# One run of full-array and one run of half-array matmuls in each mLSTM step

## The chip, the cores and the metric

The kernel runs on one core of a Trainium2 chip. The number that counts is the device time of one execution in microseconds. The engines are TensorE (PE in the rows, its weight loads PEld), VectorE (DVE), ScalarE (ACT), GpSimd (POOL) and SyncE (SP), which issues most of the transfers.

## What is computed

Three layers follow each other; only the first is touched by the change.

```python
# mLSTM: 4 batches x 8 heads, 768 time steps, head size 40
for t in range(S):
    m_new = np.maximum(f_gate[:, :, t] + m, i_gate[:, :, t])
    f_stab, i_stab = np.exp(f_gate[:, :, t] + m - m_new), np.exp(i_gate[:, :, t] - m_new)
    C = f_stab * C + i_stab * einsum('bhd,bhe->bhde', vt, kt)
    n = f_stab * n + i_stab * kt
    y[:, :, t] = sigmoid(o_gate) * (C @ qt) / max(|n . qt|, 1)
# routed layer on y as 3072 tokens of 320: 8 experts, one for each token
logits = x @ w_gate + modality_bias[modality_id]
e_idx = argmax(logits);  gate_w = softmax(logits)[e_idx]
out[mask_e] = gate_w * (relu(x[mask_e] @ w1[e]) @ w2[e])
# last layer: h = x @ w_in;  out = (h * cos(h)) @ w_out
```

## The kernel before

The recurrence is computed in chunks of 128 time steps: 6 chunks for each of 4 batches give 24 tiles of 128 tokens, and the main loop (`for i in range(NT)`, line 1070) runs over them, chunk by chunk and batch by batch. A tile holds all 8 heads in 4 pairs. The order of instructions on every engine is the order of the Python text (`manual_schedule`); the framework adds the waits. A step `i` of the loop is a software pipeline over several tiles. On TensorE it issues, in this order:

- `scores(i)`, line 459: products of queries and keys, in two groups of two head pairs. For each group two full-array matmuls (128 columns of weights, line 466) and four half-array ones (64 columns, line 472), into bank 0 for the first group and bank 1 for the second. A VectorE multiply (line 478) reads the bank of a group and follows it.
- in steps 8, 12 and 16 the count matmuls of `rank_mm` (line 656), full-array, into bank 7;
- `values(i - 1)`, line 482: the state update into bank 6 (line 491, half-array; VectorE adds it to the state in line 515), the values into bank 4 (line 498), the state's part into bank 5 (line 506; VectorE reads it in line 520). All of them are half-array;
- `spread_later(i + 2)`, line 250: the gates of a later tile, half-array, into bank 3, for ScalarE's exponentials (line 427);
- `xpose(i - 2)`, line 551: three full-array transposes of the finished tile, line 555, into bank 2;
- `logits(i - 3)`, line 560: six half-array matmuls, line 565, into columns 256 on of bank 6, read by VectorE in line 566.

A matmul of float32 leaves two records in the trace. The ranks are the tokens' places within their experts: after the tokens of a round (4 tiles, one chunk) are routed, `rank_mm(c)` counts on TensorE, and the generator `rank(c)` reads the counts on VectorE (line 677 first). Its further instructions are a background list, from which `fill()` takes one at a time at places in `scores` and `values`. Rounds 0 to 2 are ranked in steps 8, 12 and 16, round 3 through `weigh_later` in step 19, round 4 behind the loop in `first_slot`. After rounds 3 and 4 the count of each expert is left in columns 128 to 135 of the same bank, where `pick_first` and `pick_second` read it (lines 715 and 725): the two experts with the most tokens get their weights first. In steps 4, 5, 8, 9, 12 and 13 VectorE also unpacks pieces of the last layer's weights (`_decode`). SyncE loads the inputs of tile `i + 3` in step `i`; a buffer comes free when VectorE and TensorE have read it.

Of the kernel before, what the change touches and what calls it, by code (L numbers as in the profile page):

```python
# [8 lines left out]
F32 = mybir.dt.float32  # L9
# [5 lines left out]
ALU = mybir.AluOpType  # L15
# [4 lines left out]
B, H, S, D = 4, 8, 768, 40  # L20
L = 128
NC = S // L
# [3 lines left out]
NT = NTOK // 128  # L26
E = 8
# [68 lines left out]
def kernel(  # L96
# [362 lines left out]
    def scores(i):  # L459
        t = qk_t[i % NQ]  # L460
        P = st[i]
        for g in range(2):
            pairs = slice(2 * g, 2 * g + 2)
            sp = bk[g][:, 0:6 * HL].rearrange("p (n k t) -> p n k t", n=2, k=3)
            for m in range(2):
                T_.matmul(
                    out=sp[:, m, 0:2].rearrange("p k t -> p (k t)"), lhsT=t[:, 2 * g + m, HL:3 * HL],
                    rhs=t[:, 2 * g + m, QO:QO + L], start=True, stop=True,
                )
            for m in range(2):  # L470
                for a, z in enumerate(Z):
                    T_.matmul(
                        out=sp[z, m, 2], lhsT=t[:, 2 * g + m, 5 * a * HL:(5 * a + 1) * HL],
                        rhs=t[:, 2 * g + m, QO + HL:QO + L],
                        start=True, stop=True,
                    )
            pg = P[:, pairs, 0:3]
            V.tensor_tensor(out=pg, in0=sp, in1=pg, op=ALU.mult)
            if i > 1:
                fill(2)  # L480
# [78 lines left out]

    def logits(i):  # L560
        xT = xTt.pop(i)
        pl = bk[6][:, 256:256 + E] if i < NT - 2 else bk[3 if i < NT - 1 else 2][:, 0:E]
        for k in range(3):
            for z in (slice(0, 64), slice(64, 128)):
                T_.matmul(out=pl[z], lhsT=xT[:, k, z], rhs=wg[:, k, :], start=(k == 0), stop=(k == 2))
        V.tensor_tensor(out=lg[:, i, :], in0=pl, in1=bias[:, i, :], op=ALU.add)
        fill()
# [88 lines left out]
    def rank_mm(c):  # L656
        j0, n = c * B, B
        r = slice(j0, j0 + n)
        b_ = bk[7 if c < NC - 1 else 4]
        pk = b_[:, 64:64 + n * E]  # L660
        T_.matmul(out=pk, lhsT=trib[:, 0, :], rhs=oh[:, r].rearrange("p j e -> p (j e)"), start=True, stop=False)
        pk3 = pk.rearrange("p (j e) -> p j e", j=n)
        for j in range(n - 1):
            T_.matmul(
                out=pk3[:, j + 1:], lhsT=trib[:, 1, :],
                rhs=oh[:, j0 + j].unsqueeze(1).to_broadcast([128, n - 1 - j, E]), start=False, stop=False,
            )
        T_.matmul(
            out=pk3, lhsT=trib[:, 1, :], rhs=cum[:, c].unsqueeze(1).to_broadcast([128, n, E]), start=False, stop=True
        )  # L670
        if j0 + n in EARLY:
            T_.matmul(out=b_[:, 128:128 + E], lhsT=trib[:, 1, :], rhs=cum[:, c + 1], start=True, stop=True)
        return pk3

    def rank(c, pk3):
        r = slice(c * B, (c + 1) * B)
# [37 lines left out]

    def pick_first():
        r = m8[:, 1:2]
        yield from best(bk[7][:, 128:128 + E], m8[:, 0:1], r)
        V.tensor_scalar(out=tab0[:, 0:1], in0=r[0:1], scalar1=-1.0, scalar2=float(E), op0=ALU.mult, op1=ALU.add)
        yield
        V.tensor_scalar(out=star, in0=e8, scalar1=r, scalar2=None, op0=ALU.not_equal)  # L720
        yield
        V.tensor_scalar(out=s1, in0=e8, scalar1=r, scalar2=None, op0=ALU.is_equal)
        yield

    def pick_second():

        r = m8[:, 3:4]
        V.scalar_tensor_tensor(
            out=sc, in0=star, scalar=float(SLOT), in1=bk[7][:, 128:128 + E], op0=ALU.mult, op1=ALU.add
        )  # L730
        yield
        V.scalar_tensor_tensor(out=e8, in0=sc, scalar=2.0 * SLOT, in1=s1, op0=ALU.is_ge, op1=ALU.mult)
# [310 lines left out]
    def in_turn(*gs):  # L1043
        for g in gs:
            yield from g

    def weigh_later(c):
        if c < SLOW:
            wt[c] = weights(c)
            bg.append(wt[c])  # L1050
            return
        run(weights(c))
        wq.append(weigh(c))
        wt[c] = in_turn(rank(c, rank_mm(c)), rows_of(c))
        bg.append(wt[c])

    dec_ops = _decode(nc, (raw_t, dtu_t), w_in, w_out, w_ir, None, PIECES[:DA])
# [12 lines left out]
    for i in range(NT):  # L1070
# [8 lines left out]
        else:  # L1079
# [1 line left out]
            if i >= 4 and i < NT - 1 and (i - 4) % B == B - 1 and (i - 4) // B >= SLOW:  # L1081
                ex_exp((i - 4) // B)
            scores(i)
        if i >= 8 and i % B == 0 and i // B - 2 < SLOW:
            c = i // B - 2
            bg.append(in_turn(rank(c, rank_mm(c)), rows_of(c)))
        if i == NT - 2:
            run(e0)
            early_rows(0)
# [27 lines left out]
            next(gp)  # L1117
        if B <= i + 2 < NT:
            spread_later(i + 2)
        if i >= 2:  # L1120
            xpose(i - 2)
        if i >= 3:
            logits(i - 3)
        if i >= 3 and (i - 3) % B == B - 1:
            rt = route((i - 3) // B)
            bg.append(rt)
# [45 lines left out]
    twice(0)  # L1172

    def first_slot():
        rk_ = rank(NC - 2, rank_mm(NC - 2))
        bg.extend([in_turn(pick_second(), early_slot(1, sc)), in_turn(rk_, rows_of(NC - 2))])
        fill(14)
        for f in (1, 2):
            split_in(w1r, f, f, V, V, (1,))
        for _ in xpose_b(0, (4, 1, 0)):  # L1180
            fill(F0)
        for _ in range(2):
            next(we)
        split_out(w2r, 0, 0, V)
# [651 lines left out]
```

## Time and profile before

| | |
|---|---|
| median of 3 runs | 753.02 us (752.61 to 753.65) |
| the profiled execution | 751.96 us, span 750.2 us |
| TensorE busy | 719.6 us, 96% of the span |
| VectorE, ScalarE, GpSimd busy | 522.3, 387.1, 210.1 us |
| the 24 mLSTM steps | 7.75 to 151.75 us of the span |

The span runs from the first to the last instruction. In a timeline a row has its start, its duration, the engine, the line, operation and tiles, the shape of the weights (128\*128 is full-array, 128\*64 half-array) and the number of records merged; in brackets stands the idle time before it and what ended that. Spans of matmuls overlap, so their starts are to be compared, not their ends. A table by stretch has the length of a stretch, the busy time of each engine in it with the number of instructions, and the clock granted to TensorE as a share of 2.4 GHz. Steps are counted from 0; step 5 begins at 41.02 us and step 19 at 119.90.

### The profile page before, as it was taken

How to read it: one execution, taken by the hardware profiler on the slowest of the kernel's cores; microseconds unless marked ns; L12 is line 12 of the kernel's file. 1: busy time of each engine (PE TensorE's matmuls, PEld its weight loads, DVE VectorE, ACT ScalarE, POOL GpSimd, SP SyncE). 2: the span in 40 equal slices, each digit the busy share in tenths (PEclk: the TensorE clock that was granted, in tenths of full speed). 3: DMA queues.
4: the chain of work that ended last, by engine and by line, in shares of the span. 5: the costliest groups of instructions: out<-in, count | busy, mean ns of one | idle time of the engine just before them, and what ended most of it. 6: DMA issues, size and time to landing. Idle time of an engine off the chain costs nothing. (4 is left out here: it accounts for less than half of the span.)

```text
span 750.2 us, 16869 instructions
## 1 busy us (share of the span) xinstructions
PE 719.6 (96%) x6131; PEld 655.5 (87%) x6132; DVE 522.3 (70%) x1206; ACT 387.1 (52%) x910; POOL 210.1 (28%) x282
## 2 busy tenths in 40 slices
PE   8999999978999999999979999999999999999995
PEld 5888887868999999999868899998999999989994
DVE  7888888786456786773748867766767676667662
ACT  4666655463334555453736655555555555555551
POOL 7776674411344233421642002002002002001002
PEclk9999999999999999999989999999999999999998
DMA  7867877811345653423820011010010000000000
GB/s 188 220 192 206 216 211 209 249 66 54 110 125 151 206 172 98 117 71 114 267 74 1 1 35 36 1 36 36 0 36 36 1 1 36 0 1 19 18 1 35
DMA packets 45262, 68.42 MB, mean 91 GB/s; under 512 B 4846, under 2 KB 32944, under 8 KB 45168
## 3 DMA queue, kind: packets, MB, share of 16 engines
q1 hardware_dynamic: 37856, 45.16, 21.3%
q10 hardware_dynamic: 3664, 10.27, 4.7%
q0 software_dynamic: 3648, 11.82, 4.7%
q8 instruction: 49, 0.80, 0.5%
q14 instruction: 45, 0.37, 0.2%
HBM read 84.58 MB, written 12.14 MB: 129 GB/s over the span
## 5 line engine op out<-in xcount | busy, mean ns | idle before, releaser
L1648 ACT ACTIVATE w1r<-w1r 128x512 f32<-128x512 f32 x96 | 60.7, 632 | 104.3 <-DVE w1r L1643 104.3
L1650 DVE TENSOR_TENSOR w1r<-bk,w1r 128x512 f32<-128x512 f32 x96 | 66.3, 691 | 52.5 <-ACT w1r L1648 51.0
L1641 ACT ACTIVATE w1r<-bk,qtr 128x512 f32<-128x512 f32 x96 | 65.9, 687 | 57.9 <-PE bk L1636 57.8
L961 PE MATMUL bk<-XH,WIH 128*128 128x256 f32 x288 | 76.8, 296 | 1.9 <-DVEq L942 0.9
L1642 DVE TENSOR_SCALAR w1r<-w1r 128x512 f32<-128x512 f32 x96 | 41.1, 428 | 52.8 <-ACT w1r L1641 52.8
L967 ACT ACTIVATE hh<-bk 128x256 fp32r<-128x256 f32 x96 | 36.6, 381 | 77.2 <-PE bk L961 60.6
L1643 DVE TENSOR_TENSOR w1r<-w1r 128x512 f32<-128x512 f32 x96 | 68.7, 716 | 3.3
L1668 PE MATMUL bk<-WOH,gh 128*128 128x320 f32 x228 | 71.0, 311 | 0.0
L1668 PE MATMUL bk<-WOH,gl 128*128 128x320 f32 x228 | 70.5, 309 | 0.0
L1668 PE MATMUL bk<-WOL,gh 128*128 128x320 f32 x228 | 70.4, 309 | 0.0
L968 DVE SCALAR_TENSOR_TENSOR hl<-bk,hh 128x256 fp32r<-128x256 f32 x96 | 40.1, 418 | 40.9 <-ACT hh L967 29.7
L1636 PE MATMUL bk<-XH,WIH 128*128 128x512 f32 x144 | 58.3, 405 | 4.5 <-issue 3.8
L982 PE MATMUL bk<-WOH,hl 128*128 128x320 f32 x192 | 59.6, 311 | 0.9 <-DVE hl L968 0.9
L982 PE MATMUL bk<-WOH,hh 128*128 128x320 f32 x192 | 59.7, 311 | 0.0
L982 PE MATMUL bk<-WOL,hh 128*128 128x320 f32 x192 | 59.4, 309 | 0.0
L961 PEld LDWEIGHTS bk<-XH,WIH 128*128 128x128 f32 x288 | 54.8, 190 | 4.5 <-DVEq L942 3.4
L1636 PE MATMUL bk<-XL,WIH 128*128 128x512 f32 x144 | 57.8, 401 | 0.0
L988 POOL DMA_INDIRECT x_d<-ys,cinv x26 | 28.9, 1111 | 101.6 <-ACTq L942 72.5
L1636 PE MATMUL bk<-xh,WIH 128*128 128x512 f32 x144 | 56.5, 392 | 0.0
L1636 PE MATMUL bk<-xl,WIH 128*128 128x512 f32 x144 | 56.1, 389 | 0.0
L961 PE MATMUL bk<-XL,WIH 128*128 128x256 f32 x288 | 50.6, 284 | 2.7 <-DVE XL L867 2.7
L961 PE MATMUL bk<-XH,WIL 128*128 128x256 f32 x192 | 49.9, 282 | 0.0
(390 smaller groups left out, 1990.8 us busy)
## 6 DMA issues: line engine op xcount, KB each, us to landing
w2r<-in_w_dram SPq DMA_DIRECT2D x26, 640.0 KB
w1r<-in_w_dram SPq DMA_DIRECT2D x26, 512.0 KB
w1r<-in_w_dram SPq DMA_DIRECT2D x52, 128.0 KB
kvl<-in_kvn_dram SPq DMA_DIRECT2D x12, 484.0 KB
raw<-in_w_out_dram ACTq DMA_DIRECT2D x8, 640.0 KB
qkl<-in_qk_dram SPq DMA_DIRECT2D x24, 160.0 KB
x_d<-y SPq DMA_DIRECT2D x24, 160.0 KB
raw<-in_w_in_dram ACTq DMA_DIRECT2D x6, 512.0 KB
```

The source lines that it names most:

```text
L961: T_.matmul(out=ph, lhsT=a, rhs=x_, start=(n == 0), stop=(n == len(mms) - 1))
L967: A.activation(out=hh, in_=ph, func=AF.Relu)
L968: V.scalar_tensor_tensor(out=hl, in0=ph, scalar=0.0, in1=hh.bitcast(F32), op0=ALU.max, op1=ALU.subtract)
L982: T_.matmul(out=py(s, g), lhsT=a[:, gs], rhs=w_, start=(f == 0 and n == 0), stop=(f == NF - 1 and n == 2),)
L988: r = G_.indirect_dma_start(out=dst, out_offset=bass.IndirectOffsetOnAxis(ap=idx, axis=0), in_=src, in_offset=None, bounds_check=NTOK - 1, ...
L1636: T_.matmul(out=ph, lhsT=a, rhs=x_, start=(n == 0), stop=(n == len(mms) - 1))
L1641: A.activation(out=v, in_=gp[T, f], func=AF.Identity, bias=qtr, scale=1.0 / (2 * math.pi))
L1642: V.tensor_scalar(out=kk, in0=v, scalar1=MAGIC, scalar2=MAGIC, op0=ALU.add, op1=ALU.subtract)
L1643: V.tensor_tensor(out=v, in0=v, in1=kk, op=ALU.subtract)
L1648: A.activation(out=v, in_=v, func=AF.Sin, scale=6.283185)
L1650: V.tensor_tensor(out=g, in0=gp.pop((T, f)), in1=v, op=ALU.mult)
L1668: T_.matmul(out=po, lhsT=a[:, js], rhs=w_, start=(f == 0 and n == 0), stop=(f == NFC - 1 and n == 2),)
```

## The change

In `scores` the full-array matmuls of both groups go first, and then the half-array ones of both. `logits` goes ahead of `xpose`, and its output into bank 7 for tiles 2 to 20. The count matmuls of rounds 0 to 2 go behind `xpose`, and those of rounds 0 to 3 into bank 6. As bank 6 is also the state update's, the first VectorE instruction of `rank` follows the counts at once (`rank_first`), and the experts' counts are copied to a tile, `cnt`, which the picks read.

```diff
     def scores(i):
...
-        for g in range(2):
-            pairs = slice(2 * g, 2 * g + 2)
-            sp = bk[g][:, 0:6 * HL].rearrange("p (n k t) -> p n k t", n=2, k=3)
+        sps = [bk[g][:, 0:6 * HL].rearrange("p (n k t) -> p n k t", n=2, k=3) for g in range(2)]
+
+        for g, sp in enumerate(sps):
             for m in range(2):
                 T_.matmul(
                     out=sp[:, m, 0:2].rearrange("p k t -> p (k t)"), lhsT=t[:, 2 * g + m, HL:3 * HL],
                     rhs=t[:, 2 * g + m, QO:QO + L], start=True, stop=True,
                 )
+        for g, sp in enumerate(sps):
+            pairs = slice(2 * g, 2 * g + 2)
             for m in range(2):
                 for a, z in enumerate(Z):
...
     def logits(i):
         xT = xTt.pop(i)
-        pl = bk[6][:, 256:256 + E] if i < NT - 2 else bk[3 if i < NT - 1 else 2][:, 0:E]
+        if i < NT - 2:
+            pl = bk[7 if 1 < i < NT - 3 else 6][:, 256:256 + E]
+        else:
+            pl = bk[3 if i < NT - 1 else 2][:, 0:E]
...
     def rank_mm(c):
...
-        b_ = bk[7 if c < NC - 1 else 4]
+        b_ = bk[(6, 7, 4)[max(c - NC + 3, 0)]]
...
+    cnt = ra.tile([128, E], F32, name="cnt")
+
+    def rank_first(c, pk3):
+
+        g = rank(c, pk3)
+        next(g)
+        if (c + 1) * B in EARLY:
+            V.tensor_copy(out=cnt, in_=bk[6 if c < NC - 2 else 7][:, 128:128 + E])
+        return g
...
-        yield from best(bk[7][:, 128:128 + E], m8[:, 0:1], r)
+        yield from best(cnt, m8[:, 0:1], r)
...
-        wt[c] = in_turn(rank(c, rank_mm(c)), rows_of(c))
+        wt[c] = in_turn(rank_first(c, rank_mm(c)), rows_of(c))
...
             scores(i)
-        if i >= 8 and i % B == 0 and i // B - 2 < SLOW:
-            c = i // B - 2
-            bg.append(in_turn(rank(c, rank_mm(c)), rows_of(c)))
...
+        if i >= 3:
+            logits(i - 3)
         if i >= 2:
             xpose(i - 2)
-        if i >= 3:
-            logits(i - 3)
+        if i >= 8 and i % B == 0 and i // B - 2 < SLOW:
+            c = i // B - 2
+            bg.append(in_turn(rank_first(c, rank_mm(c)), rows_of(c)))
```

`pick_second` reads `cnt` in the same way, and `first_slot` calls `rank_first`. Line numbers behind `scores` grow by 2 to 15 with the change.

The order of the instructions is shown at three places, where `bk_77` and `bk_78` are banks 0 and 1, `bk_79` is bank 2, and `bk_83` and `bk_84` are banks 6 and 7. TensorE at the end of an ordinary step and the start of the next, before:

```order
L260 MATMUL bk_80<-g_108,pick 64x128
L555 MATMUL bk_79<-cst,y 128x128 x3
L565 MATMUL bk_83<-wg,xT_226 64x8 x6
L466 MATMUL bk_77<-qkl_123 128x128 x2
L472 MATMUL bk_77<-qkl_123 64x64 x4
L466 MATMUL bk_78<-qkl_123 128x128 x2
L472 MATMUL bk_78<-qkl_123 64x64 x4
L491 MATMUL bk_83<-kvl_124,kw_107 64x41 x8
```

and the same place after:

```order
L260 MATMUL bk_80<-g_108,pick 64x128
L570 MATMUL bk_84<-wg,xT_226 64x8 x6
L557 MATMUL bk_79<-cst,y 128x128 x3
L466 MATMUL bk_77<-qkl_123 128x128 x2
L466 MATMUL bk_78<-qkl_123 128x128 x2
L474 MATMUL bk_77<-qkl_123 64x64 x4
L474 MATMUL bk_78<-qkl_123 64x64 x4
L493 MATMUL bk_83<-kvl_124,kw_107 64x41 x8
```

The six matmuls of the logits moved past the transposes and into bank 7, and between the gates' last matmul and the state update there is now one run of each shape. TensorE in step 16, with the counts of round 2, before:

```order
L472 MATMUL bk_78<-qk_111 64x64 x4
L661 LDWEIGHTS trib
L661 MATMUL bk_84<-oh,trib 128x32
L664 LDWEIGHTS trib
L664 MATMUL bk_84<-oh,trib 128x24
L664 LDWEIGHTS trib
L664 MATMUL bk_84<-oh,trib 128x16
L664 LDWEIGHTS trib
L664 MATMUL bk_84<-oh,trib 128x8
L668 LDWEIGHTS trib
L668 MATMUL bk_84<-cum,trib 128x32
L491 MATMUL bk_83<-kvl_125,kw_105 64x41 x8
```

and after:

```order
L570 MATMUL bk_84<-wg,xT_226 64x8 x6
L557 MATMUL bk_79<-cst,y 128x128 x3
L666 LDWEIGHTS trib
L666 MATMUL bk_83<-oh,trib 128x32
L669 LDWEIGHTS trib
L669 MATMUL bk_83<-oh,trib 128x24
L669 LDWEIGHTS trib
L669 MATMUL bk_83<-oh,trib 128x16
L669 LDWEIGHTS trib
L669 MATMUL bk_83<-oh,trib 128x8
L673 LDWEIGHTS trib
L673 MATMUL bk_83<-cum,trib 128x32
```

The counts moved from behind the scores to the end of the step and from bank 7 to bank 6. VectorE between steps 19 and 20, from the last instruction of the round's weights to the state update, before:

```order
L613 RECIPROCAL gate<-gate 128x4
L478 TENSOR_TENSOR Pl_129<-bk_77,Pl_129 128x2x192
L677 TENSOR_TENSOR tot<-bk_84,oh 128x32
L706 TENSOR_REDUCE m_254<-bk_84 128x1
L478 TENSOR_TENSOR Pl_129<-bk_78,Pl_129 128x2x192
L679 TENSOR_REDUCE rk<-tot 128x4
L708 SCALAR_TENSOR_TENSOR e_255<-bk_84,m_254,cst 128x8
L515 TENSOR_TENSOR Ml_131<-Mc_215,bk_83 40x4x41 x2
```

and after:

```order
L618 RECIPROCAL gate<-gate 128x4
L692 TENSOR_TENSOR tot<-bk_83,oh 128x32
L687 COPY cnt<-bk_83 128x8
L480 TENSOR_TENSOR Pl_129<-bk_77,Pl_129 128x2x192
L694 TENSOR_REDUCE rk<-tot 128x4
L721 TENSOR_REDUCE m_255<-cnt 128x1
L480 TENSOR_TENSOR Pl_129<-bk_78,Pl_129 128x2x192
L696 TENSOR_SCALAR hF<-rk 128x4
L723 SCALAR_TENSOR_TENSOR e_256<-cnt,m_255,cst 128x8
L517 TENSOR_TENSOR Ml_131<-Mc_215,bk_83 40x4x41 x2
```

The read of the counts moved ahead of the scores' multiplies, and the copy to `cnt` stands behind it.

## Rows read from the trace of the kernel before

**Rows 1.** Busy time by stretch, steps 3 to 23; columns as described above.

```profile
28.30:41.02 12.72, 12.72 (x196) 10.89 (x195) 8.74 (x21) 8.74 (x28) 10.06 (x16) 0.89 0.70 198
41.02:63.36 22.34, 22.15 (x421) 19.41 (x418) 17.71 (x56) 12.70 (x48) 15.53 (x26) 1.00 0.71 202
63.36:86.00 22.64, 22.40 (x421) 19.53 (x417) 19.68 (x67) 13.91 (x50) 15.31 (x24) 1.00 0.80 222
86.00:108.66 22.66, 22.42 (x422) 19.54 (x418) 19.71 (x67) 13.39 (x48) 15.76 (x25) 1.00 0.77 207
108.66:119.90 11.24, 11.10 (x210) 9.64 (x206) 7.79 (x29) 6.74 (x25) 7.45 (x13) 1.00 0.75 202
119.90:133.16 13.26, 11.15 (x216) 9.73 (x212) 12.17 (x43) 6.96 (x25) 4.40 (x8) 1.00 0.80 222
133.16:151.75 18.59, 17.19 (x266) 15.00 (x262) 13.43 (x55) 8.12 (x28) 7.51 (x11) 0.91 0.88 252
```

**Rows 2.** Waits, 41.02 to 119.90: who for whom, total, times, longest (us).

```profile
DVE Ml L515 <- PE bk L506: 6.7, 6, 1.4
...
DVE M L515 <- PE bk L506: 4.6, 3, 1.6
...
PEld bk L491 <- DVE lg L566: 0.5, 3, 0.2
```

**Rows 3.** VectorE's waits, 63.36 to 86.00.

```profile
DVE Ml L515 <- PE bk L506: 2.2, 2, 1.4
```

**Rows 4.** Timeline of TensorE, step 18.

```profile
114.41 0.71 PE L466 MATMUL bk<-qkl 128*128 128x128 f32 x4
115.05 0.45 PE L472 MATMUL bk<-qkl 128*64 128x64 f32 x8
...
116.07 0.45 PE L472 MATMUL bk<-qkl 128*64 128x64 f32 x8
116.36 0.62 PE L491 MATMUL bk<-kvb,kw 128*64 128x41 f32 x16
...
118.85 0.55 PE L555 MATMUL bk<-cst,y 128*128 128x128 f32 x3
119.45 0.52 PE L565 MATMUL bk<-wg,xT 128*64 128x8 f32 x12
119.90 0.71 PE L466 MATMUL bk<-qkl 128*128 128x128 f32 x4
```

**Rows 5.** Timeline of TensorE, small windows: scores of step 17; the last gate matmul.

```profile
108.87 0.50 PE L466 MATMUL bk<-qkb 128*128 128x128 f32 x3
109.09 0.28 PE L466 MATMUL bk<-qkb 128*128 128x128 f32 x1
...
118.70 0.22 PE L260 MATMUL bk<-g,pick 96*64 96x128 bf16 x1
```

**Rows 6.** Line 466, 41 to 120: its weight loads, ns minimum/median/maximum.

```profile
L466 PEld LDWEIGHTS bk<-qkl x57: 186/189/192, 46.5 to 119.9; 128*128 128x128 f32 x57
```

**Rows 7.** Timeline of TensorE behind the loop: transposes, then a full-array matmul.

```profile
155.25 0.55 PE L555 MATMUL bk<-cst,y 128*128 128x128 f32 x3
155.55 0.37 PE L961 MATMUL bk<-XH,WIH 128*128 128x256 f32 x1
```

**Rows 8.** Timeline of VectorE between steps 19 and 20.

```profile
128.77 0.18 DVE L613 RECIPROCAL gate<-gate 128x4 f32<-128x4 f32 x1
...
130.72 0.66 DVE L515 TENSOR_TENSOR Ml<-Mc,bk 40x164 f32<-40x164 f32 x2 [0.45 <-PE bk L506]
```

**Rows 9.** Timeline of TensorE: step 20, scores of step 21, the last values.

```profile
128.34 0.62 PE L491 MATMUL bk<-kvl,kw 128*64 128x41 f32 x16
...
133.16 0.93 PE L466 MATMUL bk<-qkb 128*128 128x128 f32 x4
...
136.28 1.40 PE L498 MATMUL bk<-vb,Pl 128*64 128x82 f32 x21
...
151.75 1.14 PE L498 MATMUL bk<-vbl,Pl 128*64 128x82 f32 x21 [1.40 <-DVE lg L566]
```

More of the change, by code (lines that the diff above doesn't have):

```diff
@@ L728, in pick_second @@
         V.scalar_tensor_tensor(
-            out=sc, in0=star, scalar=float(SLOT), in1=bk[7][:, 128:128 + E], op0=ALU.mult, op1=ALU.add
+            out=sc, in0=star, scalar=float(SLOT), in1=cnt, op0=ALU.mult, op1=ALU.add
         )
@@ L1174, in first_slot @@
     def first_slot():
-        rk_ = rank(NC - 2, rank_mm(NC - 2))
+        rk_ = rank_first(NC - 2, rank_mm(NC - 2))
         bg.extend([in_turn(pick_second(), early_slot(1, sc)), in_turn(rk_, rows_of(NC - 2))])
```

## The prediction

> **What bounds the kernel now.** The change touches only the first fifth of the program, the 24 mLSTM steps, so I read the busy time by stretches first [rows 1]: in each stretch the reader is to set TensorE's busy time beside the length. From 41.02 to 119.90 us (steps 5 to 18) TensorE is busy for 22.15 of 22.34, 22.40 of 22.64, 22.42 of 22.66 and 11.10 of 11.24 us, at the full 2.4 GHz (granted clock 1.00). These steps are as long as TensorE's instructions are. VectorE is next: 17.71, 19.68, 19.71 and 7.79 us. The second and third stretch hold the steps in which VectorE also unpacks the late weights; there little is free on it. In 119.90 to 133.16 (steps 19 and 20) VectorE leads instead, 12.17 against 11.15 of 13.26.
>
> Second, the waits of VectorE, since they say how much of a TensorE gain it can follow. From 41.02 to 119.90 it waits for one thing, the matmuls of line 506, for 6.7 + 4.6 = 11.3 us [rows 2]; 2.2 us of that fall into 63.36 to 86.00 [rows 3], and the next stretch, 86.00 to 108.66, has the same busy time.
>
> Third, the timeline of TensorE in step 18, where nothing but the order of shapes costs time [rows 4]. The step lasts 119.90 - 114.41 = 5.49 us. Its scores take 116.36 - 114.41 = 1.95 us: a group of full-array matmuls 0.64 (115.05 - 114.41), a group of half-array ones, the same again, the last half-array group, which more half-array work follows, only 0.29. Inside a full-array group the pitch is small: its second record starts at 108.87 and its fourth at 109.09, so 0.11 us each [rows 5]. The rest of the 0.64 is paid on the way in and out of the group.
>
> **The change part by part.**
>
> *Scores.* The two full-array groups become one of eight records and the two half-array groups one of eight pairs. The first takes 0.64 + 4 x 0.11 = 1.08 us. The second takes 0.29 plus four more pairs at no more than 0.29 / 4 = 0.07; inside a run I take 0.06, so 0.24. Sum 1.61 against 1.95: 0.34 us less in each step, 0.29 at the least.
>
> A weight load of these matmuls takes 186 to 192 ns [rows 6], longer than the 0.11 us pitch, so it runs beside the matmul before it. The Trainium skill (TensorE: Matmul & The Clock Gate, Part 3, "The mechanism") says that a weight load overlaps running matmuls only where their row groups differ, which full-array ones never do. By that rule the four added records would cost 4 x 0.19 and the scores would gain 0.02 instead of 0.34; the pitch in the trace speaks against it, and I go by the pitch.
>
> *Logits ahead of the transposes.* Now: last gate-spreading matmul 118.70 [rows 5], transposes 118.85, logits 119.45, next scores 119.90 [rows 4]; 1.20 us. The logits start 0.60 after three transposes that elsewhere need 155.55 - 155.25 = 0.30 until a full-array matmul follows them [rows 7]. After the change: logits one half-array pitch behind the spreading (0.06), 0.45 from them to the transposes (what they take to the next full-array matmul now), 0.30 to the scores: 0.81. Saved 0.39. Part of it is a wait and not a switch: the logits share bank 6 with the state update, which line 515 reads, and the own bank (7) ends that. Together a step falls by 0.73, from 5.49 to 4.76 us.
>
> *The count matmuls of the ranks* (line 661 on) go behind the transposes into the same full-array run, and into bank 6. That saves TensorE one more pair of switches in steps 8, 12 and 16; I count nothing, since VectorE binds in two of the three. In return the next step's state-update matmuls (line 491) must wait until line 677 has read bank 6. They already wait for the logits' read in three steps (0.5 us in all [rows 2]); line 677 now stands right behind that read, so the wait goes on by one short instruction, 0.1 us each: 0.3 in all.
>
> *What VectorE lets through.* TensorE's gain per stretch of four steps is 4 x 0.73 = 2.9. Steps 5 to 8: VectorE leaves 22.34 - 17.71 = 4.6 free, so 2.9 arrive. Steps 9 to 12: it waits only 2.2, so 2.2 is the cap; steps 13 to 16 the same. Steps 17 and 18: 2 x 0.73 and 0.2 for a wait for the logits' read that goes, 1.7, against 3.4 free. Sum 9.0, less the 0.3: 8.7. Steps 3 and 4 (28.30 to 41.02, VectorE busy for 8.74 of 12.72) give 0.34 each and about 0.3 each for the end of the step, 1.2.
>
> *Steps 19 and 20.* VectorE is the chain; TensorE's gain is worth nothing here. And here the shared bank costs: the copy to cnt and line 677 stand right behind line 613, which ends at 128.77 + 0.18 = 128.95 [rows 8]. The state-update matmuls, at 128.34 now [rows 9], cannot start before about 129.25 (two short instructions): 0.9 later. Behind them on TensorE stand the value matmuls and line 506, for which VectorE waits 0.45 already at 130.72. VectorE has the two instructions behind it by then, so I charge 0.6; the bounds are 0 and 0.9.
>
> *Steps 21 to 23.* 133.16 to 151.75 has TensorE busy for 17.19 of 18.59 and VectorE for 13.43. TensorE gains 3 x 0.73 = 2.2, of which I count 2.0. At its end the last value matmuls wait 1.40 us for the logits' read of bank 6 [rows 9]; that goes with the bank. What is late next there is VectorE, which has the routing of the last full round in front of its own read of these matmuls; of the 1.40 I count 1.0. Sum 3.0. The bounds: 0, if the gather or the weights loaded here land late (the transfers fill 0.88 of 18.59, 16.4 us, which leaves 2.2 to gain if they had to end first), and 4.6, with all of the 1.40 and VectorE never late.
>
> The sum is 1.2 + 8.7 - 0.6 + 3.0 = 12.3 us. The second cnt copy and the new SBUF tile are under 0.2 and inside the rounding. From the routing on the program is unaltered and moves forward as a whole. The profiled execution took 751.96 us with a span of 750.2; that gives 739.7. It lies 1.1 under the median shown, 753.02, and from the median it would be 740.7. I say 740.
>
> **The rivals.**
>
> *VectorE cannot trail.* To fill its 1.4 us wait for line 506 it must run that much later behind TensorE; but the scores of the next step need the banks that it reads. If it can't, one such wait stays in each of the stretches 41.02 to 108.66: 3 x 1.4 = 4.2, less what the first has to spare (4.6 - 2.9 = 1.7), 2.5, and as much as 4.2. The gain is then 8.1 to 9.8, the time about 743. For it: the wait stands in every rank step. Against: scores take 1.6 of 4.8 us, so a bank has some 3 us to be read.
>
> *TensorE's gain arrives whole.* VectorE's instructions in the unpacking steps close up, or its lag is carried into steps 17 and 18, where it has 1.7 to spare: 12.3 + 1.7, and with the 0.6 not lost 14.6. Time 737.4. Against it: 19.7 of 22.64 us are busy time, which doesn't shrink.
>
> *The weight loads show* (by the rule of the skill above). The scores gain nothing, a step 0.39: 14 x 0.39 = 5.5, with 2.2 at the end (3 x 0.39 and 1.0) and 0.6 at the start less 0.6 in step 20, 7.7. Time 744.
>
> *TensorE loses its clock: slower.* A TensorE that waits briefly for VectorE in every step may be clocked down. The row that has it: in steps 21 to 23 the granted clock is 0.91 on average, and the scores of step 21 take 136.28 - 133.16 = 3.12 us [rows 9] against 1.95 in step 18, with the 1.2 GHz level in it, 1.2 us dearer. The place is steps 9 to 18, where the waits will be; from eleven such falls on the 12.3 are used up, with fourteen (16.8) the time is some 756.5. Against: all of steps 5 to 18 hold 1.00, with TensorE 98% busy, and a VectorE-bound step of about 5.1 us would still have TensorE busy for 4.76. The Trainium skill (the same page, "A second HAM failure mode: psum-queue depth-cycling") describes this: short idles between groups of matmuls, clock up and down; no stretch of steps 5 to 18 shows it.
>
> *Nothing comes of it*: the gain is eaten by waits for bank 6 in four places. It would take 3 us in each; 752.
>
> **How the numbers follow.** Forecast 0.52; VectorE cannot trail 0.24; the gain whole 0.12; the loads show 0.04; the clock 0.05; nothing 0.03. What one can tell from no change here is about 0.2%, 1.5 us: faster 0.92, the same 0.03, slower 0.05. The unknown terms are 0.29 to 0.34 per step of scores, 0 to 0.9 in step 20, 0 to 4.6 at the end, and 2.2 to 3.1 in each of the two VectorE-bound stretches. The range, 735 to 746, takes in the second, third and fourth case and leaves out about one in seven.
>
> **What would show it.** Right: in a step's timeline eight records of the scores' full-array matmuls in a row at 0.11, start of scores to start of line 491's matmuls about 1.6; logits right behind the gate spreading; the step at about 4.8 in steps 5 to 8 and 17 to 18, about 5.1 in 9 to 16 with VectorE busy for over 95%; no wait of 1.40 before the last value matmuls; a wait of TensorE for the cnt copy in step 20. Wrong: steps of 5.4 or more; waits of VectorE for line 506 that stay at 1.4; granted clocks under 1.00 between steps 5 and 18; a late gather after step 23.

## The result and the profile after

Timed beside the kernel before, the changed kernel takes 745.55 us in the median of 4 runs (745.15 to 747.41), the kernel before 752.82: 7.3 us less, a ratio of 0.9903. The ratio on record is 0.9872, 95% interval 0.9837 to 0.9907, which is 7.0 to 12.3 us less; it is not the ratio of these medians, and the times behind it are not listed. The profiled execution took 745.15 us with a span of 743.5, 6.8 less than before. The forecast was 740, with a gain of 12.3: the sign and the range hold, and by the medians and the two profiles some 5 us of the gain are missing (by the interval, 0 to 5). The profiles say where.

The busy time by stretches, for the same steps as in [rows 1]: stretch and its length, then busy us of PE, PEld, DVE, ACT and POOL, TensorE's granted clock, DMA share, GB/s.

```profile
28.67:39.21 10.54, 10.54 (x198) 9.68 (x197) 8.93 (x19) 8.39 (x27) 9.13 (x14) 1.00 0.85 231
39.21:58.89 19.68, 19.15 (x420) 18.40 (x418) 18.57 (x57) 12.66 (x46) 15.69 (x25) 1.00 0.75 211
58.89:80.10 21.21, 19.81 (x423) 18.60 (x420) 20.27 (x67) 13.93 (x48) 16.22 (x25) 1.00 0.87 228
80.10:102.19 22.09, 19.96 (x423) 18.72 (x420) 21.19 (x66) 13.39 (x46) 16.10 (x25) 1.00 0.79 223
102.19:112.47 10.28, 9.67 (x212) 9.25 (x209) 8.42 (x28) 6.74 (x23) 7.49 (x13) 1.00 0.82 230
112.47:126.16 13.69, 10.18 (x215) 9.42 (x213) 11.88 (x41) 7.08 (x24) 5.86 (x10) 1.00 0.79 224
126.16:142.84 16.68, 15.42 (x263) 14.65 (x261) 12.47 (x49) 6.79 (x23) 7.34 (x10) 0.90 0.76 236
```

TensorE gained nearly what it was to gain: 19.81 and 19.96 us of work in the third and fourth row against 22.40 and 22.42, 2.5 us less, where 2.9 were forecast. But these stretches fell only to 21.21 and 22.09 from 22.64 and 22.66. VectorE, which was busy for 19.68 and 19.71 us in them, now is for 20.27 and 21.19: its own busy time grew, though the change gives it only two small copies, both behind these stretches. The fifth row shows the same, 8.42 against 7.79.

The waits in the same steps as [rows 2], 39.21 to 112.47 (engine and line, who for whom: us in total, times, longest):

```profile
PE bk L493 <- DVE tot L692: 1.8, 3, 0.6
DVE M L517 <- PE bk L508: 1.8, 3, 0.9
PE bk L260 <- ACT Pl L427: 1.4, 2, 0.7
...
PE bk L500 <- DVE hq L526: 0.4, 1, 0.4
PE bk L466 <- DVE Pl L480: 0.3, 1, 0.3
```

VectorE's waits for TensorE, 11.3 us before, are down to 1.8 (line 517 is 515 of before, line 508 is 506), and TensorE now waits for others, with the reads of the ranks first. The roles have changed.

One step without disturbance, step 18, in the timeline of TensorE, to be laid beside [rows 4]:

```profile
107.78 1.06 PE L466 MATMUL bk<-qkl 128*128 128x128 f32 x8
108.77 0.69 PE L474 MATMUL bk<-qkl 128*64 128x64 f32 x16
109.29 0.62 PE L493 MATMUL bk<-kvb,kw 128*64 128x41 f32 x16
...
111.64 0.51 PE L570 MATMUL bk<-wg,xT 128*64 128x8 f32 x10
112.09 0.55 PE L557 MATMUL bk<-cst,y 128*128 128x128 f32 x3
112.47 0.39 PE L466 MATMUL bk<-qkl 128*128 128x128 f32 x2
```

The eight full-array records begin 0.11 us apart and are over in 0.99 (108.77 - 107.78), the half-array ones in 0.52. The scores take 1.51 us where they took 1.95. The logits begin among the last gate matmuls, with no gap; the transposes follow, and 0.38 later the next scores. The step lasts 112.47 - 107.78 = 4.69 us against 5.49.

Four more places in the same timeline: step 9, step 20, step 22 and the end of the loop.

```profile
61.25 0.67 PE L493 MATMUL bk<-kv,kw 128*64 128x41 f32 x16 [0.61 <-DVE tot L692]
...
122.39 0.67 PE L493 MATMUL bk<-kvl,kw 128*64 128x41 f32 x16 [1.46 <-DVE cnt L687]
...
133.50 1.21 PE L815 MATMUL bk<-Bq,Oq 128*128 128x4 bf16 x16 [1.09 <-DVE lg L571]
...
142.84 1.14 PE L500 MATMUL bk<-vbl,Pl 128*64 128x82 f32 x21
```

The wait of 1.40 before the last value matmuls [rows 9] is gone. Two came: the forecast one for the copy of the counts in step 20, and one that nobody had foreseen in step 22, where the slot matmuls (line 815) write bank 7, which the logits now use too.

### The profile page after: what moved, and what is told of

Its sections match the earlier page's. It is cut to its first block, busy times and chain, and to the rows that moved or that the text cites. A ratio compares the mean times of both kernels' runs of the same rounds, so it can differ in the third digit from the quotient of the medians.

```text
span 743.5 us, 16872 instructions
## 1 busy us (share of the span) xinstructions
PE 705.6 (95%) x6132; PEld 650.3 (87%) x6132; DVE 527.9 (71%) x1208; ACT 386.8 (52%) x910; POOL 214.9 (29%) x282
## 5 line engine op out<-in xcount | busy, mean ns | idle before, releaser
L1003 POOL DMA_INDIRECT x_d<-ys,cinv x26 | 30.7, 1182 | 99.8 <-ACTq L957 70.6
```

Source lines behind the costliest of these rows:

```text
L1003: r = G_.indirect_dma_start(out=dst, out_offset=bass.IndirectOffsetOnAxis(ap=idx, axis=0), in_=src, in_offset=None, bounds_check=NTOK - 1, ...
```

## The experiments

A step is taken from the first record of one tile's scores to that of the next, in the timeline of TensorE. "Steps 5 to 18" is the time from the scores of tile 5 to those of tile 19: 78.88 us before (41.02 to 119.90), 73.26 after (39.21 to 112.47). Those steps handle the same tiles in every kernel, and TensorE runs at 2.4 GHz in all of them (granted clock 1.00). There is one profile of each kernel. Two kernels that hold the same instructions in these steps (the ranks in bank 5, and the banks, both below) took 72.84 and 73.26, so 0.4 us between two profiles cannot be told from nothing. Nor can 1.8 us ahead of step 5: three kernels that are the same up to there began it at 39.21 (the changed kernel), 37.44 and 37.96.

### The scores alone

```diff
 (the kernel before)
-        for g in range(2):           # four full-array records, eight half-array ones, twice
+        for g, sp in enumerate(sps): # eight full-array records
+            ...
+        for g, sp in enumerate(sps): # sixteen half-array records
```

> The kernel before with the merged score groups alone (logits, transposes, ranks and banks as before). Theory, VectorE is full and what the new order costs it eats the rest: TensorE's step falls by the 0.45 us that the scores save in the trace of after (1.95 to 1.50), VectorE can follow that almost everywhere (4 x 0.45 = 1.8 against the 2.2 it has free in steps 9 to 12 and 13 to 16), so the start of step 19 moves forward by about 6.5 us, nearly the 7.4 of the whole change, and the time is 745 to 746.5. Rival, the two parts simply add up, each with its share of TensorE's 0.8 us per step: 0.45 / 0.81 of 7.3 = 4.1 us, 748.7. Rival, weight loads show in the run of eight full-array matmuls: no gain, 752.

Measured: ratio 0.9919 (0.9887 to 0.9951). But steps 6 and 7 take 5.57 and 5.54 us, no less than before, and steps 5 to 18 take 78.29. The theory fails, and so does the rival that shares the gain out. The waits of these steps:

```profile
PEld bk L493 <- DVE lg L568: 3.6, 8, 0.8
...
PE bk L493 <- DVE lg L568: 2.3, 6, 0.7
```

The state-update matmuls now come so early that they wait for the logits' read of bank 6. What the scores save is handed to that wait. The total fell at other places: 1.7 us before step 5, no more than such profiles differ by, and in step 21, which takes 4.56 us at full clock instead of 6.39 at 0.73. On the scale of 752.8 the ratio is 746.7 us, close to the theory's time, but not for the theory's reason.

### The order alone

```diff
 (the changed kernel)
-        for g, sp in enumerate(sps):  # merged scores
+        for g in range(2):            # the two groups of before
```

> The changed kernel with the scores in their old four groups (logits ahead of the transposes, bank 7, ranks in bank 6 behind the transposes stay). TensorE's step is 5.49 - 0.36 = 5.13 us. Theory (VectorE full, its work lengthened by the new order): steps 5 to 8 and 17, 18 gain 0.36 each, 2.2 in all, steps 9 to 16 about 2, scores of step 19 some 4.5 us earlier, 0.4 lost in steps 19 and 20, 1 to 2 more at the end: time 747 to 749.5. Rival, the parts add up: 0.36 / 0.81 of 7.3 = 3.2 us, 749.6; by that rival this run and the one with the scores alone make 7.3 together, by the theory 9 to 12, since each alone leaves VectorE free and both together don't.

Measured: ratio 0.9946 (0.9922 to 0.9969). Steps 6 and 7: 5.03 us each; steps 5 to 18: 75.24. The step is 0.10 shorter than expected, and the 0.34 from here to 4.69 is what the merged scores are worth once bank 6 does not hold them back. The theory expected the two parts alone to make more than the whole, 9 to 12 us. By the ratios they make 6.1 + 4.1, but not in the steps that the theory spoke of: in steps 5 to 18 they bring 0.6 and 3.6, less than the 5.6 of the whole.

### The order against the bank

```diff
 (the changed kernel)
-        if i >= 3: logits(i - 3)
         if i >= 2: xpose(i - 2)
+        if i >= 3: logits(i - 3)      # behind the transposes, still in bank 7
```

> The changed kernel with the logits again behind the transposes, but still in their own bank 7; scores merged, ranks last. It parts the order from the bank. Theory, a switch between half and full arrays costs 0.15 to 0.2 us wherever it stands: two more switches, steps 6 and 7 at 4.69 + 0.27 to 0.39 = 4.96 to 5.08, start of step 19 some 2 us later than 112.5 (VectorE hides part), time 747 to 748. Rival, the bank was what mattered: steps 6 and 7 stay under 4.8, time as the changed kernel. The run with the scores alone (steps at 5.54, line 493 waiting for the logits' read of bank 6) lets me expect that the bank is worth at least as much as the order.

Measured: ratio 0.9896 (0.9864 to 0.9929); steps 6 and 7: 5.03 us; steps 5 to 18: 75.24. The order is worth 0.34 us a step, inside the range expected.

### The bank alone

```diff
 (the changed kernel)
-        for g, sp in enumerate(sps):  # merged scores
+        for g in range(2):            # the two groups of before
...
         if i >= 2: xpose(i - 2)
+        if i >= 3: logits(i - 3)      # behind the transposes, still in bank 7
```

> The changed kernel with the scores in four groups and the logits behind the transposes, both as before; what is left of the change is the logits' own bank and the ranks behind the transposes in bank 6. Completes the table of parts, for steps 6 and 7: before 5.49, scores alone 5.54, order with bank 5.03, scores with bank 5.03, all 4.69. If the parts add once the bank is free, 5.03 + 0.34 = 5.37 here: the bank is worth 0.12, and 0.46 more as soon as the scores are merged. Rivals: 5.49, the bank alone is worth nothing; 5.03, the bank is everything and the two others pay only together.

Measured, one run: steps 6 and 7 take 5.37 us each, as the sum has it; 747.3 us. The table of parts is then whole:

| logits' bank | order | scores | step 6, 7 (us) | steps 5 to 18 (us) |
|---|---|---|---|---|
| 6 | old | two groups (before) | 5.49 | 78.88 |
| 6 | old | merged | 5.57, 5.54 | 78.29 |
| 7 | old | two groups | 5.37 | 76.25 |
| 7 | old | merged | 5.03 | 75.24 |
| 7 | new | two groups | 5.03 | 75.24 |
| 7 | new | merged (after) | 4.69 | 73.26 |

With its own bank each part is worth 0.34 us in a step that VectorE does not hold, and they add up. Without it the merged scores are worth nothing there. Over steps 5 to 18 the parts bring 1.0 or 2.0 us instead of 14 x 0.34 = 4.8, which again points at VectorE.

### The unpacking late

```diff
-STEPS = (2, 2)
+STEPS = (0, 0)        # all twelve unpacking instructions at the end of step 22
```

> The changed kernel with all twelve VectorE instructions that unpack the late weights moved from steps 4 to 13 to the end of step 22. Only the starts of steps up to 19 are meant to be read; step 22 grows by some 9.6 us. Theory, VectorE is the bound of steps 8 to 16: without these 9.6 us it has room and every step takes what steps 5 to 7 take now, 4.70, the three rank steps 0.25 more, so step 19 starts 14 x 4.70 + 0.75 = 66.5 us behind step 5 instead of 73.3. Rival, the waits for bank 6 and for the exps in the rank steps (0.61 + 0.6 each) are a bound by themselves: the rank steps stay at about 5.9, the others at 4.7, 69.4 us. Rival, something on TensorE (loads, switches): 73 us as now.

Measured: steps 5 to 18 take 69.08 us, 4.2 less. VectorE was the bound there. But it is not 66.5: steps without ranks take 4.69, steps 9, 13 and 17 take 5.52, 5.60 and 5.50. The number is the rival's. The next two runs ask why.

### The ranks in another bank

```diff
-        b_ = bk[(6, 7, 4)[max(c - NC + 3, 0)]]
+        b_ = bk[(5, 7, 4)[max(c - NC + 3, 0)]]   # and cnt is copied from bank 5
```

> Both: unpacking at the end of step 22, counts of the ranks in bank 5. To be compared with the run that has the unpacking late alone, where step 5 to step 19 take 69.08 and steps 9, 13 and 17 take 5.50 to 5.60 against 4.69 in steps without ranks, though VectorE has room. Theory, that 0.85 us is the wait of line 493 for the read of bank 6: these three steps fall to 4.7 to 4.8, the three rank steps before them rise by about 0.3, step 5 to 19 take 67.5 to 67.9. Rival, it is VectorE's own lag (the rank's instructions push everything back): the wait moves to line 508 or to the scores of the next step and 69 us remain.

Measured, with the unpacking late: 67.50 us; steps 9, 13 and 17 take 4.77, the rank steps before them 5.23, 0.1 to 0.4 longer. The waits, first with the counts in bank 6, then in bank 5:

```profile
PE bk L493 <- DVE tot L692: 1.7, 3, 0.6
```

```profile
PE bk L666 <- DVE hq L522: 0.3, 1, 0.3
```

So the wait is the bank's, and it costs 69.08 - 67.50 = 1.6 us when VectorE has room.

> The changed kernel with the count matmuls of the ranks in bank 5 (the state read's) in place of bank 6, order as changed. Line 493 then waits for no read of a rank; in exchange the counts wait for VectorE's read of bank 5 (line 522), some 0.3 us in each rank step. Theory A, VectorE is full from step 8 to 17 (it has no idle time there) and only the late-unpacking run is bound by the bank: the wait goes and another comes, steps 5 to 18 together stay within 0.5 us of 73.3. Theory B, the wait for bank 6 (line 493 starts 0.86 us later in steps 9, 13 and 17 than in the others) is paid in full: 3 x (0.86 - 0.3) = 1.7 us less, 71.6. In both, step 20 loses its 1.7 us wait of line 493 for the cnt copy, of which VectorE's chain lets 0 to 0.6 through. Time: A 745 to 746 on the scale where the changed kernel has 745.5 and the kernel before 752.8 (ratio 0.990), B ratio 0.987 less 0.002 to 0.003.

Measured, with the unpacking where it was: steps 5 to 18 take 72.84, 0.4 less, which is theory A and no more than two profiles differ by. A full VectorE hides that wait, for it would have made TensorE wait somewhere else. Steps 19 and 20 grew from 13.69 to 14.90 us. In step 19, 0.5 longer, the count of rank 3 now waited 2.2 us for line 522, after 1.7 for line 517 in the changed kernel. In step 20, 0.7 longer, the granted clock was 0.59; the run above, with the same wait of 2.2 and a granted clock of 1.00, took 13.67 for both steps. Ratio 0.9857 (0.9828 to 0.9886). That is nearer to theory B's, but of the 4.1 us between the two profiled executions 1.8 lie before step 5 and 3.2 behind the loop, where the two kernels are the same.

### GpSimd's products left out

```diff
-            G_.tensor_tensor(out=kw_t[i % 3][:, :, :, 0:D], ...)      # line 440
-                    G_.tensor_tensor(out=Mc[b][r], ...)               # line 450
...
-                    V.tensor_tensor(out=m_, in0=Mc[b][r], in1=ps[r], op=ALU.add)
+                    V.tensor_tensor(out=m_, in0=m_, in1=ps[r], op=ALU.add)
```

> Leaves out two GpSimd products of each step (the weighted keys and the decayed state; the state update adds to the state itself), so the state is wrong; everything else is the changed kernel. Theory, VectorE's instructions without a PSUM operand are stretched while GpSimd runs these products: line 540 falls from 0.38 beside GpSimd to 0.16, line 533 from 0.66 to 0.49, the ranks' lines 696, 700, 705 from 0.23 to 0.34 to 0.16, the unpacking's 1769 from 1.09 to about 0.68; instructions that read PSUM (480, 517, 522, 526) stay. VectorE's work per round of four steps falls by 1 to 1.5 us, and so do steps 9 to 16: step 5 to 19 take 70 to 71.5 instead of 73.3. Rival, the spread of these durations has another cause (the operands' layout, DMA writes into the same memory): they stay, and so does 73.3 within 0.5.

First VectorE's costliest instructions of steps 5 to 18 by line: shapes, count, busy us, mean ns. Before:

```profile
L478 DVE TENSOR_TENSOR Pl<-bk,Pl 128x384 f32<-128x384 f32 x18 | 9.5, 547 | 0.0
...
L531 DVE SCALAR_TENSOR_TENSOR y<-kvl,hq 128x320 f32<-128x320 f32 x6 | 2.9, 491 | 0.0
...
L538 DVE SCALAR_TENSOR_TENSOR den<-hq 128x8 f32<-128x8 f32 x13 | 2.1, 164 | 0.0
...
L681 DVE TENSOR_SCALAR hF<-rk 128x4 f32<-128x4 f32 x3 | 0.5, 162 | 0.0
```

The changed kernel:

```profile
L480 DVE TENSOR_TENSOR Pl<-bk,Pl 128x384 f32<-128x384 f32 x18 | 9.6, 544 | 0.0
...
L540 DVE SCALAR_TENSOR_TENSOR den<-hq 128x8 f32<-128x8 f32 x14 | 4.3, 309 | 0.0
L533 DVE SCALAR_TENSOR_TENSOR y<-kvl,hq 128x320 f32<-128x320 f32 x6 | 3.9, 644 | 0.1
...
L696 DVE TENSOR_SCALAR hF<-rk 128x4 f32<-128x4 f32 x3 | 1.0, 344 | 0.1
```

Without the two products (lines are 13 less):

```profile
L467 DVE TENSOR_TENSOR Pl<-bk,Pl 128x384 f32<-128x384 f32 x18 | 9.6, 546 | 0.1
L520 DVE SCALAR_TENSOR_TENSOR y<-kvl,hq 128x320 f32<-128x320 f32 x6 | 3.0, 492 | 1.0 <-DMA x_d<-y 0.9
...
L527 DVE SCALAR_TENSOR_TENSOR den<-hq 128x8 f32<-128x8 f32 x13 | 2.1, 165 | 0.0
...
L683 DVE TENSOR_SCALAR hF<-rk 128x4 f32<-128x4 f32 x3 | 0.7, 240 | 0.1
```

The denominators' instruction went from 164 to 309 ns with the change and is at 165 without the products; `y` from 491 to 644 and back to 492. The multiply of the scores, which reads PSUM, stays at 546 in all three. VectorE's busy time in steps 5 to 18, third number of the first group:

```profile
41.02:119.90 78.88, 78.07 (x1461) 68.11 (x1457) 64.89 (x213) 46.73 (x165) 54.05 (x85) 1.00 0.76 209
```

```profile
39.21:112.47 73.26, 68.59 (x1459) 64.97 (x1458) 68.46 (x215) 46.72 (x163) 55.50 (x85) 1.00 0.80 222
```

```profile
38.16:109.42 71.26, 68.05 (x1459) 64.70 (x1458) 64.41 (x213) 46.90 (x163) 31.07 (x43) 1.00 0.87 228
```

64.89 before, 68.46 after, 64.41 without the products, and the steps are 2.0 us shorter: the growth of VectorE's work comes from running beside them. The 71.26 holds another wait, ahead of tile 12's scores, which the changed kernel doesn't have (TensorE's timeline, and the waits of SyncE's queue):

```profile
74.38 0.35 PE L453 MATMUL bk<-qk 128*128 128x128 f32 x1 [1.55 <-DVE ex L587]
```

```profile
SPq L231 <- DMA qk<-in_qk_dram: 1.1, 1, 1.1
```

The row names a VectorE instruction that the scores do not read. What they read is `qk`, the input of tile 12, and SyncE's queue waited for the landing of the same input until 74.27. Without these 1.55 us the run would have taken as little as 69.7.

The expectation missed in two instructions: an unpacking one stays at 1.09 us, and the ranks' short ones do not simply fall: line 696 goes from 344 to 240 ns, line 705 from 234 to 295. Both still run beside GpSimd instructions that this run leaves in, the unpacking one beside the product for `y` and the ranks' beside line 436. Of the three instances of line 705 (692 here) two run alone, in 161 and 163 ns; the third starts 0.10 us behind the first of a pair of line 436 and ends 0.01 us behind it:

```profile
102.93 0.65 POOL L436 TENSOR_SCALAR_AFFINE_SELECT P<-P 64x512 f32<-64x512 f32 x1 [0.75 <-ACT P L427]
103.03 0.56 DVE L692 SCALAR_TENSOR_TENSOR qB<-hL,rk 128x4 bf16<-128x4 bf16 x1
```

One pair from the timeline of the changed kernel, step 13:

```profile
80.42 0.72 POOL L440 TENSOR_TENSOR kw<-kvb,aw 128x320 f32<-128x320 f32 x1
80.62 0.87 DVE L533 SCALAR_TENSOR_TENSOR y<-kvl,hq 128x320 f32<-128x320 f32 x1
81.10 1.27 POOL L450 TENSOR_TENSOR Mc<-M,decay 40x164 f32<-40x164 f32 x2
81.41 0.43 DVE L540 SCALAR_TENSOR_TENSOR den<-hq 128x8 f32<-128x8 f32 x1
81.88 0.17 DVE L542 TENSOR_SCALAR den<-den 128x8 f32<-128x8 f32 x1
```

An instruction on 8 elements per partition takes 0.43 us beside the state's product and the next one 0.17. Line 538 of before ran with no GpSimd instruction beside it in all of its 13 instances of steps 5 to 18; of the 13 that start in these steps after the change (line 540) 7 run beside a product, for 311 to 432 ns, and each ends 0.03 us behind the product. The Trainium skill (SBUF — State Buffer, "SBUF: two separate sides") says that VectorE and GpSimd share one pair of SBUF ports under an exclusive lock: a VectorE instruction takes it in a two-port mode, or with two SBUF inputs against a GpSimd instruction that reads SBUF, and whichever starts first holds it to its end while the other waits. The trace agrees: lines 533 and 540 have two such inputs and stretch, line 480 has one and one in PSUM and does not. Lines 696 and 700 have one input, in SBUF, and stretch too; no run here shows in which mode they ran.

### Attempts at a faster kernel

```diff
 (the unpacking where VectorE has room, in the changed kernel)
-STEPS = (2, 2)
+UNPACK = {4: 2, 5: 2, 6: 2, 7: 1, 17: 1, 18: 2, 21: 1}
```

> The changed kernel with the twelve unpacking instructions taken out of steps 8, 9, 12 and 13 and put where VectorE has room: steps 4, 5, 6 (two each), 7 (one), 17 (one), 18 (two), 21 (one), 22 (the last). Theory (VectorE is the bound of 8 to 16): these steps fall to about 4.75, 3 to 4 us up to step 19, of which the later steps give back up to 1: time 742 to 743.5. Rival (waits for bank 6 and for the exps bind): under 1 us gained, 744.5 to 746. Slower only if the end of step 22 waits for the unpacking, as the gather stands behind it.

Measured: ratio 0.989 (0.9856 to 0.9924), no better than the changed kernel. Steps 5 to 18 gained 0.6 us only: steps 10 to 12 and 14 shortened, but step 8 took 7.25 us, and steps 19 and 20 took 15.53 instead of 13.69, with a wait of 2.83 us for line 517 ahead of the counts and a granted clock of 0.62 in step 20.

```diff
 (the changed kernel; further runs build on this)
-        b_ = bk[(6, 7, 4)[max(c - NC + 3, 0)]]
+        b_ = bk[5 if c < SLOW else (6, 7, 4)[c - NC + 3]]
-            pl = bk[7 if 1 < i < NT - 3 else 6][:, 256:256 + E]
+            pl = bk[7 if 1 < i < NT - 6 or i == NT - 4 else 6][:, 256:256 + E]
```

> The changed kernel with the counts of ranks 0 to 2 in bank 5, the count of rank 3 left in bank 6, and the logits of tiles 18 and 19 in bank 6, which nobody else uses by then, so that the slot matmuls of step 22 (line 815, bank 7) no longer wait 1.1 us for VectorE's read of the logits. Against the run with all four ranks in bank 5: step 5 to 19 the same 72.8; steps 19 and 20 back from 14.9 to the 13.7 of the changed kernel (rank 3 waited 2.2 us for line 522 there); the 1.1 us in step 22 gone. Scores of step 23 at 135.5, and 134.3 if TensorE's slow stretch in step 22 goes with that wait. Time 739 to 742 where before has 752.8, ratio 0.982 to 0.986. Rival, VectorE's chain of steps 19 to 22 sets their length and not TensorE's waits: scores of step 23 at 137 or later, ratio as the changed kernel's.

Measured: the scores of step 23 start at 134.86 us (138.70 in the changed kernel) and the first routed tokens are split at 145.80 (149.50). The trace holds what was expected there; steps 5 to 18 took 73.26, though, with a wait of 1.47 us ahead of tile 12's scores, again for the tile's input. The ratio, 0.9865 (0.983 to 0.990), is above what was expected and cannot be told from the changed kernel's. Steps 21 and 22 of the changed kernel and of this one:

```profile
126.16:130.74 4.58, 4.41 (x90) 4.10 (x88) 4.55 (x18) 3.60 (x12) 2.03 (x4) 1.00 0.61 188
130.74:138.70 7.96, 6.87 (x97) 6.72 (x96) 4.76 (x19) 2.70 (x10) 4.59 (x6) 0.79 0.70 202
```

```profile
124.92:129.51 4.59, 4.41 (x89) 4.10 (x88) 4.55 (x18) 3.60 (x12) 2.03 (x4) 1.00 0.56 179
129.51:134.86 5.35, 5.35 (x97) 5.12 (x96) 4.15 (x18) 2.70 (x10) 2.35 (x4) 1.00 0.66 197
```

Step 22 takes 2.6 us less: the wait of 1.09 for the logits' read is gone, and with it the stretch at 1.2 GHz that the mean clock of 0.79 holds. Not all of that is kept: in this run the granted clock is 0.50 from 144.4 to 151.0 us, behind the loop, and in the changed kernel from 135.5 to 138.7 and again from 152.5 to 155.8.

```diff
 (on top of the banks)
+            A.activation(out=den, in_=hq[:, :, D:DV], func=AF.Abs)   # behind the sum, line 526
-        V.scalar_tensor_tensor(out=den, in0=nq, scalar=-1.0, in1=nq, op0=ALU.mult, op1=ALU.max)   # stays for tiles 0 to 3
```

> The same with one VectorE instruction of each step (line 540, the absolute value of the denominators, 0.31 us on average because it is stretched beside GpSimd's products) given to ScalarE, issued behind the state read's sum. Theory (VectorE full in steps 8 to 17): 0.3 us less in each of these ten steps, step 5 to 19 take 70 to 71 instead of 72.8, ratio 0.003 to 0.004 below the run with the banks alone. Rival, ScalarE, whose queue is in order, now waits for VectorE ahead of the copies that the logits need: no gain, or 1 to 3 us lost.

Measured: the rival. Steps 5 to 18 take 75.05 us; ratio 0.9857 (0.9825 to 0.9888). ScalarE waits in its queue for VectorE's sum, and TensorE for the exponentials behind it (waits of steps 5 to 18):

```profile
ACT den L528 <- DVE hq L526: 24.4, 12, 3.2
PE bk L260 <- ACT Pl L427: 4.0, 5, 1.4
```

```diff
 (on top of the banks)
-DA = 3
+DA = 1                                  # early pieces; the others in the expert steps
+            if f == NF - 1: next(dec[0], None)
```

> The kernel of the run with the banks (counts 0 to 2 in bank 5, logits of tiles 18 and 19 in bank 6), with only the first of the three early pieces unpacked in steps 4 and 5; the other two (eight VectorE instructions, 6.4 us, four of them each in steps 8, 9 and 12, 13 before) go to the expert steps between 198 and 333 us, where TensorE is busy for 132.7 of 135 us and VectorE for 65. Theory (VectorE's own work is what holds steps 8 to 17): step 5 to 19 take 67.5 to 68.5, as in the run with the unpacking late and the counts in bank 5, instead of 73.3; the scores of step 23 start at 129 to 131 instead of 134.9; the expert steps lose 0 to 1 us; time 736 to 739, ratio 0.978 to 0.982. Rivals: the gather and the weights loaded in step 22 are late by then and hold the start of the experts (their matmuls already wait 3.4 us for the gather with the banks alone): 1 to 2 us gained; or the experts pay for the added unpacking: ratio as with the banks alone, 0.9865.

Measured: steps 5 to 18 take 69.26 us, 4.0 less than with the banks alone but 0.8 over the range. TensorE waits that long for the input of tile 16:

```profile
93.77 0.35 PE L466 MATMUL bk<-qk 128*128 128x128 f32 x1 [0.83 <-DMA qk<-in_qk_dram]
```

Step 20 took 8.53 us, at a granted clock of 0.60, after 6.99 at 1.00 with the banks alone, and the scores of step 23 start at 133.70, 1.2 earlier. Ratio 0.9898 (0.9861 to 0.9935). The execution took 599.5 us from the first routed tokens to its end, against 590.5 to 597.7 in the profiles of all the other kernels, so the experts may have paid for the unpacking. That spread, among kernels with nearly the same program there, is too wide to settle it with one profile.

No kernel here is shown to beat the changed one.

## Why the prediction was right, and where it was not

| steps | forecast gain | measured gain |
|---|---|---|
| up to step 4 | 1.2 | 1.8 |
| 5 to 8 | 2.9 | 2.65 |
| 9 to 12 | 2.2 | 1.4 |
| 13 to 16 | 2.2 | 0.6 |
| 17 and 18 | 1.7 | 1.0 |
| 19 and 20 | -0.6 | -0.4 |
| 21 to 23 and the last wait | 3.0 | 1.4 |
| behind the loop | 0 | -1.6 |
| sum | 12.6, less 0.3 for the ranks' reads: 12.3 | 6.8 |

The measured column compares the two profiled executions, by the starts of the scores and, for its last two rows, by the read of tile 23's state (line 520, now 522) at 153.71 and 145.32. The 1.8 up to step 4 cannot be put down to the change, as kernels that are the same up to there differ by as much.

- *TensorE's step.* Right: 4.69 against 4.76, scores 1.51 against 1.61. The pitch of 0.11 us holds in a run of eight. By the rule that the prediction cited from the Trainium skill (TensorE: Matmul & The Clock Gate, Part 3, "The mechanism"; the section also lets a load be pulled ahead into a background weight buffer, a case that the prediction left out), eight loads of 186 ns or more [rows 6] one behind the other would have taken 1.5 us; the run took 0.99. The saving from the logits, 0.39, was 0.46: 0.34 the order, 0.12 the bank.
- *"What VectorE lets through".* This step failed, in the size of its terms. The cap of 2.2 us in steps 9 to 16 was read from VectorE's waits, and the prediction said against the larger gain that busy time "doesn't shrink". It did not ask whether it can grow. It grew by 3.6 us over steps 5 to 18, as the new order laid VectorE's instructions on two SBUF tiles beside GpSimd's products more often. Of the 3.1 us missing there the run without the products gives back 2.0, and up to 3.5 if its wait for an input is set aside (with GpSimd freer as well, which the run does not part from it). So the 3.1 need no other cause, but one profile does not show that there is none.
- *The reads of the ranks.* "0.1 us each" was wrong: line 493 starts 0.86 us later in steps 9, 13 and 17 than in steps without ranks. In steps 5 to 18 the run without it was 0.4 us shorter, no more than two profiles differ by, because VectorE is full; with room on VectorE it costs 1.6.
- *Steps 19 and 20.* Right: the wait for the copy is 1.46 us and the two steps lost 0.43.
- *Steps 21 to 23.* The wait of 1.40 went, as said, and from the scores of step 23 to the read of its state 1.5 us were gained. Step 22 lost 1.9, by a wait that the prediction did not see, line 815 for bank 7, and the clock that fell behind it: 2.6 us together, as the run with the banks shows. Step 21 gained 1.8, not the forecast 0.7. In the kernel before its granted clock is 0.73, so part of it runs at 1.2 GHz (the row below); in all the other kernels here it is 1.00. The prediction read the dear scores of that step [rows 9] and did not ask whether the fall would stay. Why it went no run shows: that part of the gain was not forecast, and its cause stays open.

```profile
133.16:139.55 6.39, 6.39 (x91) 5.54 (x87) 5.18 (x21) 3.60 (x13) 2.50 (x4) 0.73 0.80 234
```

- *Behind the loop.* The -1.6 is no effect of the change that can be shown: from the first routed tokens to the end it takes 590.5 to 599.5 us in the other profiles, 592.8 before and 594.0 after.
- *The rivals.* "VectorE cannot trail" gave about 743, near the result, but by a mechanism that did not come: its waits for the state read went from 11.3 to 1.8 us. The gain did not arrive whole, the weight loads do not show, and the clock held 1.00 in steps 5 to 18. It did fall, once, in step 22.

## What to carry to other kernels

Before a bank is shared or freed, ask which read of it ends last: the same edit was worth 0.34 us a step with a bank of its own and nothing without. When an engine is near full, its busy time before is no cap for after: look for instructions whose durations differ between occurrences, and for the engine that runs beside the long ones. And look at every writer of the bank that takes in the moved tile, down to the one-off work at the loop's end. Before two profiles are compared, set aside the waits for an input and the stretches at the lower clock that only one of them has.

## What the hardware showed

- A VectorE instruction on 8 elements per partition with both inputs in SBUF (line 540) takes 157 to 169 ns alone in the changed kernel. Beside a GpSimd product it takes 311 to 687 ns and ends 0.03 us behind the product, in all ten instances.
- In step 22 the six kernels in which TensorE waited 0.7 to 1.1 us for bank 7 ahead of line 815 (the changed kernel among them) had a mean granted clock of 0.79 to 0.80 and took 7.87 to 8.09 us. The eight others, with no such wait or a shorter one, had 1.00 and took 5.35 to 6.18. Such a wait alone does not decide it: behind waits of 1.71 us in step 19 and 0.8 in step 20, step 20 had a granted clock of 0.60 in two kernels (those with the unpacking late and with part of it in the expert steps), and behind 1.71 and 1.46 us it had 1.00 in the changed kernel.
